# Splitting the cast of the token values and re-ordering the matrix engine in a segmented transformer with memory

## The chip, the cores and the metric

The kernel runs on one core of a Trainium2 chip. The metric is the device time of one execution in microseconds (us). A core has five engines that run in parallel and meet at semaphores: TensorE (PE, with its weight loads shown apart as PEld), VectorE (DVE), ScalarE (ACT), GpSimd (POOL) and SyncE (SP). Here SP issues nearly all of the DMAs.

## The reference

The input x has 2048 rows of 512. Attention goes through it in 64 segments of 32 tokens, one after the other, because the 8 memory rows of a segment are the first 8 output rows of the one before:

```python
for s in range(n_seg):                               # 64
    h = concat([mem, xs])                            # 8 + 32 rows of 512
    q, k, v = (einsum('btd,dhe->bhte', h, W) for W in (Wq, Wk, Wv))   # 32 heads of 128
    p = softmax(where(mask, q @ k^T * scale, -1e9))
    o = einsum('bhte,hed->btd', p @ v, Wo)
    mem = o[:, :8]; outs.append(o[:, 8:])
h  = x + A(layernorm(x))
h2 = h + gelu(layernorm(h) @ w1 + b1) @ w2 + b2      # inner size 1792
```

## The kernel before, in words

**Work of a segment on PE.** The query and key passes of both halves of the heads (Q0, Q1, K0, K1) and the value passes (V0, V1) come from `one_pass` (line 796 and, with a weight that is still loaded, line 547). Each is written in four units of four matmuls of 128x512. SC0 and SC1 are the scores of the memory rows (line 963), PV0 and PV1 their values (lines 994 and 998), PVA the values of the 24 token rows of the segment before (line 1055). WO is the output projection in eight units of eight matmuls (`wo_units`, line 1083); in a trace it is 64 matmuls. SA is the scores of token rows (line 1025). F0 and F1 are fillers: passes of a block of 4 segments whose results are needed later (hB is the tile that they read, line 796), or the output projection of a block's last rows (`wo_B`, line 1112, tile OTB, eight units of four matmuls).

**The order.** `ORDERS` is a table of strings that gives, for each place, the order of these units on PE. The places are a1 to a3 (the first segments), m0 to m3 (the segments between by their number modulo 4) and z60 to z63 (the last). "F1.0.3" stands for units 0 to 2 of F1. `TURNED` names passes that run through their four blocks backwards, so that a weight can be kept from one pass to the next. DVE, ACT, POOL and SP get their order from a list scheduler in which `BONUS` shifts priorities; it also picks ACT or DVE for operations declared with `either`. `LOCK`, `LEAD` and `PADS` insert weight loads so that instruction fetches come at set places.

**The recurrence.** WO's last matmul is followed by a transpose of its PSUM bank on DVE (tile TT, line 1095), two additions that write the memory rows into hT (line 1089), and the first Q or K matmul of the next segment, which reads them. What the table writes behind WO in a segment (fillers and SA) runs on PE beside this chain; what it writes between the first hT matmul and WO's end does not.

**Token values.** PVA leaves its result in PSUM in the tile quad; `pv_a_ev` (lines 1060 to 1064) copies it into OT with one cast of 128x768, under the key OTx. All eight WO units of a segment wait for that key.

**The start.** Lines 710 to 724 issue the first DMAs: memory rows, the bias and two blocks of x on ACT's queue, and on SP's queue WV, WK and WQ in four pieces of 1 MB each and WO in eight pieces of 512 KB. A normalised block of x is the tile xn (line 738), made on DVE from statistics (line 734) and a reciprocal root on POOL (rst, lines 736 and 737). From the third block on xn is made during the segments, one in four segments. oBn (line 1120) is a sum on DVE of the token rows of a block, also one in four segments. The statement that records it is marked `alone`, which makes the next instruction on DVE be preceded by a wait.

Of the kernel before, what the change touches and what calls it, by code (L numbers as in the profile page):

```python
# [1599 lines left out]
```

## Time and profile before

| | |
|---|---|
| median of 3 runs | 806.18 us (803.99 to 807.5) |
| the profiled execution | 803.95 us, of which its span is 802.2 us |
| mean granted PE clock | 0.998 |
| busy in the span: PE, DVE, ACT, POOL | 97%, 75%, 70%, 11% |
| DMA | 48.77 MB, 61 GB/s over the span |

In the profile a row of the timeline has the start, the time from the start of its first instruction to the end of its last, engine and line, the tiles and how many instructions are run together. The end of a matmul is modelled: rows of PE overlap, so times on PE are taken below from start to start. A bracket behind a row is idle time ahead of it and what ended it. A window row holds each engine's busy time and the clock that PE was granted.

### The profile page before, as it was taken

How to read it: one execution, taken by the hardware profiler on the slowest of the kernel's cores; microseconds unless marked ns; L12 is line 12 of the kernel's file. 1: busy time of each engine (PE TensorE's matmuls, PEld its weight loads, DVE VectorE, ACT ScalarE, POOL GpSimd, SP SyncE). 2: the span in 40 equal slices, each digit the busy share in tenths (PEclk: the TensorE clock that was granted, in tenths of full speed). 3: DMA queues.
4: the chain of work that ended last, by engine and by line, in shares of the span. 5: the costliest groups of instructions: out<-in, count | busy, mean ns of one | idle time of the engine just before them, and what ended most of it. 6: DMA issues, size and time to landing. Idle time of an engine off the chain costs nothing.

```text
span 802.2 us, 46835 instructions
## 1 busy us (share of the span) xinstructions
PE 775.9 (97%) x21699; PEld 423.1 (53%) x20880; DVE 600.7 (75%) x1847; ACT 558.0 (70%) x1580; POOL 90.1 (11%) x211
## 2 busy tenths in 40 slices
PE   2899999999999999999999999999999999999998
PEld 1455555555555555555555555555555555644444
DVE  3277878888888888888888888888888888732311
ACT  1557777777777777777778777777777777773342
POOL 5022000010001010101010101000000000020700
PEclk9999999999999999999999999999999999999999
DMA  9961010201111121102010202010212112074300
GB/s 367 394 174 24 4 37 11 45 12 37 26 33 30 30 33 27 36 19 42 19 43 15 49 12 50 13 37 20 50 25 56 51 38 59 17 232 127 86 27 26
DMA packets 65555, 48.77 MB, mean 61 GB/s; under 512 B 28996, under 2 KB 63308, under 8 KB 63820
## 3 DMA queue, kind: packets, MB, share of 16 engines
q1 hardware_dynamic: 65024, 45.50, 20.3%
q8 instruction: 166, 2.72, 1.4%
q14 instruction: 33, 0.27, 0.1%
q10 hardware_dynamic: 332, 0.27, 0.1%
HBM read 31.08 MB, written 8.13 MB: 49 GB/s over the span
## 4 chain that ended last, share of the span: by engine, by line
PE 91%; DMA 3%; DVE 2%; ACT 1%; SPq 1%; issue 1%; POOL 0%; DVEq 0%; ACTq 0%
PE ps L796 43%; PE ps L1083 15%; PE ps L547 8%; PE quad L1465 6%; PE ps L1451 5%; DMA WQ<-in_A_Wq_dram 3%; PE ps L1112 3%; PE quad L994 3%; PE quad L1055 2%; PE ps L1025 2%; PE ps L1233 1%; PE ps L963 1%; PE quad L963 1%; SPq L708 1%; PE quad L998 1%
## 5 line engine op out<-in xcount | busy, mean ns | idle before, releaser
L1083 PE MATMUL ps<-WO,OT 128*32 128x256 bf16 x4224 | 140.6, 274 | 0.1
L796 PE MATMUL ps<-WQ,hT 128*32 128x512 bf16 x1864 | 131.6, 379 | 0.7 <-DVE hT L1089 0.5
L796 PE MATMUL ps<-WV,hT 128*32 128x512 bf16 x1364 | 125.2, 381 | 0.0
L796 PE MATMUL ps<-WK,hT 128*32 128x512 bf16 x1700 | 123.6, 380 | 0.1
L815 ACT ACTIVATE kq<-ps 128x512 bf16<-128x512 f32 x160 | 95.4, 597 | 32.3 <-PE ps L796 26.4
L1083 PEld LDWEIGHTS ps<-WO,OT 128*32 128x32 bf16 x4224 | 100.9, 96 | 26.5 <-ACT OT L814 5.5
L814 ACT CAST kq<-ps 128x512 bf16<-128x512 f32 x162 | 94.8, 585 | 19.9 <-PE ps L796 13.1
L814 ACT CAST OT<-quad 128x128 bf16<-128x128 f32 x191 | 84.4, 442 | 27.0 <-PE quad L998 18.8
L839 DVE STREAM_TRANSPOSE KALL<-kq 128x256 f32<-128x256 f32 x160 | 71.2, 445 | 15.0 <-ACT kq L814 11.8
L796 PEld LDWEIGHTS ps<-WQ,hT 128*32 128x32 bf16 x1864 | 50.3, 97 | 58.8 <-issue 19.0
L861 POOL COPY ZC<-QTB 128x256 bf16<-128x256 bf16 x64 | 25.6, 401 | 477.2 <-PE ps L963 455.7
L796 PEld LDWEIGHTS ps<-WK,hT 128*32 128x32 bf16 x1700 | 45.8, 96 | 56.9 <-issue 14.5
L547 PE MATMUL ps<-WV,hT 128*32 128x512 bf16 x684 | 67.6, 379 | 0.0
L796 PEld LDWEIGHTS ps<-WV,hT 128*32 128x32 bf16 x1364 | 38.4, 97 | 47.3 <-issue 36.6
L839 DVE STREAM_TRANSPOSE QT<-kq 128x256 f32<-128x256 f32 x128 | 57.0, 445 | 6.5 <-ACT kq L815 1.9
L1454 ACT ACTIVATE WQ<-ps,b1t 128x512 bf16<-128x512 f32 x42 | 28.9, 688 | 46.6 <-PE ps L1451 46.6
L1095 DVE STREAM_TRANSPOSE TT<-ps 128x256 f32<-128x256 f32 x66 | 29.7, 450 | 36.3 <-PE ps L1083 36.1
L814 ACT CAST VS<-ps 128x512 bf16<-128x512 f32 x65 | 38.1, 586 | 26.6 <-PE ps L796 26.5
L814 DVE CAST VS<-ps 128x512 bf16<-128x512 f32 x63 | 41.8, 663 | 5.4 <-PE ps L796 5.4
L1541 DVE TENSOR_TENSOR WV<-quad,WV 128x512 bf16<-128x512 f32 (+1 forms) x16 | 10.5, 672 | 45.6 <-PE quad L1465 45.6
L982 DVE TENSOR_TENSOR PC<-EC,rsc 128x128 bf16<-128x128 f32 x128 | 39.7, 310 | 4.3
L1112 PE MATMUL ps<-WO,OTB 128*32 128x512 bf16 x512 | 42.1, 381 | 0.4 <-issue 0.2
(163 smaller groups left out, 1432.1 us busy)
## 6 DMA issues: line engine op xcount, KB each, us to landing
WV<-in_A_Wv_dram SPq DMA_DIRECT2D x4, 1024.0 KB, 8.5
WK<-in_A_Wk_dram SPq DMA_DIRECT2D x4, 1024.0 KB, 14.2
WQ<-in_A_Wq_dram SPq DMA_DIRECT2D x4, 1024.0 KB, 24.7
WO<-in_A_Wo_dram SPq DMA_DIRECT2D x8, 512.0 KB, 9.4
v_last<-VSB SPq DMA_DIRECT2D x60, 64.0 KB, 2.9
VBD<-v_last SPq DMA_DIRECT2D x60, 64.0 KB, 2.9
h_mid<-xr SPq DMA_DIRECT2D x16, 128.0 KB, 1.8
WK<-in_B_w_dram SPq DMA_DIRECT2D x4, 512.0 KB, 4.6
```

What stands on the lines that cost most here:

```text
L547: return e.add_instruction(mybir.InstMatmult(name="I-%d" % (4000000 + _kept[0]), engine=mybir.EngineType.PE, start_tensor_calc=start, stop ...
L796: ins = e.matmul(o, l, m, start=(k == 0), stop=(k == DC - 1), tile_position=(0, 32 * j), skip_group_check=True)
L814: return {"act": (lambda e: e.copy(out, src), t_act(n, ps_)), "dve": (lambda e: e.tensor_copy(out, src), 0.16 + 1.042e-3 * n * fast)}
L815: return {"act": (lambda e: e.mul(out, src, scale_), t_act(n, ps_)), "dve": (lambda e: e.tensor_scalar(out, src, scale_, None, ALU.mult), ...
L839: S.op("dve", lambda e: e.transpose(out, src), reads=[("kq", i)], writes=[key], dur=t_dve(256) + 0.02, after=after)
L982: S.op("dve", lambda e: e.tensor_tensor(PC[:, r].rearrange("p t a -> p a t"), EC[:, r], bc, ALU.mult), reads=[("EC", r), ("rsc", r)], writ ...
L1083: ins = e.matmul(ps[bank][32 * j:32 * j + 32, 0:256], lhs(slot(h)), wo_cols(h, b), start=(k == 0), stop=(k == 15), tile_position=(0, 32 * ...
L1095: S.op("dve", lambda e: e.transpose(tt.rearrange("p c q t -> p (c q t)"), ps[bank][:, 0:256]), reads=[("ps", bank)], writes=[("TT", par)], ...
L1112: ins = e.matmul(ps[bank][32 * j:32 * j + 32, :], OTB[:, bk % 2, slot(h), :], WO[:, h, :], start=(k == 0), stop=(k == 7), tile_position=(0 ...
L1451: ins = e.matmul(ps[bank][:, 0:SBT], W1[:, cc, fc * P:(fc + 1) * P], hnT_of(k)[:, cc, :], start=(cc == 0), stop=(cc == DC - 1))
L1454: S.op("act", lambda e: e.activation(gT[:, fc, :], ps[bank][:, 0:SBT], ACTF.Gelu_apprx_tanh, bias=b1t[:, fc:fc + 1], scale=1.0), reads=[(" ...
L1465: S.op("pe", lambda e: e.matmul(quad[:, t, :], lhs, W2[:, fc, :], **flags), reads=[("W2", part_of(fc))] + gT_keys(k, fc), writes=[("ps", t ...
```

## The change

1. `pv_a_ev` makes two casts of 128x384, one for each half of the heads, under the keys (OTx, half); a WO unit waits only for the half it reads.
2. WO is loaded in 16 pieces of 256 KB, and a WO unit waits only for its own two. Both blocks of x are now issued ahead of the memory rows and the bias, and these four issues are held in that order.
3. `ORDERS`, `TURNED` and `BONUS` are new throughout; LOCK is 108 for 106, LEAD 189 for 199.

```diff
-LOCK = 106
+LOCK = 108
-LATE, RAW, LEAD = 0, 12, 199
+LATE, RAW, LEAD = 0, 12, 189
...
-          "m3": "K0.0.1 Q0.0.2 K0.1.2 Q0.2.4 K0.2.4 Q1.0.4 K1.0.4 SC0.0.1 V1.0.1 V0.0.1 V1.1.2 V0.1.3 V1.2.3 V0.3.4 SC1.0.1 F1.0.1 V1.3.4 PVA.0.2 PV0.0.1 F1.1.5 WO.0.1 PV1.0.1 WO.1.8 F1.5.7 SA.0.1 F1.7.8",
+          "m3": "K0.0.1 Q0.0.2 K0.1.2 Q0.2.4 Q1.0.1 K0.2.4 Q1.1.4 K1.0.4 SC0.0.1 V1.0.1 V0.0.2 V1.1.3 V0.2.4 SC1.0.1 V1.3.4 F1.0.1 PVA.0.2 PV0.0.1 F1.1.4 WO.0.2 PV1.0.1 WO.2.8 F1.4.7 SA.0.1 F1.7.8",
...
         def first(fn, kb, writes):
-            S.dma(fn, kb, writes=writes, eng="act")
+            firsts.append(S.dma(fn, kb, writes=writes, eng="act", behind=firsts[-1] if firsts else None))
+        firsts = []
         load_x(0, first)
+        load_x(1, first)
         first(lambda e: e.dma_start(m0, A_mem0[0]), 8, ["m0"])
         first(lambda e: e.dma_start(b1n[:], b1_d), 4, ["b1n"])
-        load_x(1, first)
...
-        for g in range(4):
+        for q in range(8):
             for a in range(2):
-                h0 = 16 * (g // 2) + 8 * a + 4 * (g % 2)
-                load(lambda e, h0=h0: e.dma_start(WO[:, h0:h0 + 4, :], wo_d[:, h0:h0 + 4, :]), 590, [("WO", g, a)])
+                h0 = 16 * (q // 4) + 8 * a + 2 * (q % 4)
+                load(lambda e, h0=h0: e.dma_start(WO[:, h0:h0 + 2, :], wo_d[:, h0:h0 + 2, :]), 295, [("WO", q, a)])
...
         def pv_a_ev(s):
             opar = s % 2
-            src = quad[:, :, 256:512].rearrange("p j (k q) -> p j k q", k=8)[:, :, :, 0:NA]
-            ot = OT[:, opar, :, 0:NA].rearrange("p (j k) q -> p j k q", k=8)
-            S.either(copy2(ot, src, 768), reads=QK, writes=[("OTx", opar)])
+            for half in range(2):
+                k = slice(4 * half, 4 * half + 4)
+                src = quad[:, :, 256:512].rearrange("p j (k q) -> p j k q", k=8)[:, :, k, 0:NA]
+                ot = OT[:, opar, :, 0:NA].rearrange("p (j k) q -> p j k q", k=8)[:, :, k]
+                S.named(S.either(copy2(ot, src, 384), reads=QK, writes=[("OTx", opar, half)]), "OTx%d" % half)
...
-                S.op("pe", f, reads=[("WO", q // 2, a) for a in range(2)] + reads(q // 4), writes=[("ps", bank)], dur=0.22, mode=MC, ni=16)
+                S.op("pe", f, reads=[("WO", q, a) for a in range(2)] + reads(q // 4), writes=[("ps", bank)], dur=0.22, mode=MC, ni=16)
...
-            wo_units(lambda sl: OT[:, par, sl, :], lambda r: [("OTm", par, r), ("OTx", par)], bank)
+            wo_units(lambda sl: OT[:, par, sl, :], lambda r: [("OTm", par, r), ("OTx", par, r)], bank)
```

**The end of m3 on PE.** From PVA of an m3 segment to the last instruction ahead of the next segment's first matmul on hT, the instructions of before stand like this (a row is a run of equal instructions; WO,OTB is the filler `wo_B`, WO,OT the projection WO, KALL,QT is SA):

```order
L1055 MATMUL quad<-PTA,VS 128x32 x32
L994 MATMUL quad<-PTC,VS 128x16 x16
L998 MATMUL quad<-PTC,VBD 128x64 x4
L1112 MATMUL ps<-WO,OTB 32x512 x16
L1083 MATMUL ps<-WO,OT 32x256 x8
L994 MATMUL quad<-PTC,VS 128x16 x16
L998 MATMUL quad<-PTC,VBD 128x64 x4
L1083 MATMUL ps<-WO,OT 32x256 x56
L1112 MATMUL ps<-WO,OTB 32x512 x8
L1025 MATMUL ps<-KALL,QT 32x32 x32
L1112 MATMUL ps<-WO,OTB 32x512 x4
```

The same place of the changed kernel:

```order
L1058 MATMUL quad<-PTA,VS 128x32 x32
L997 MATMUL quad<-PTC,VS 128x16 x16
L1001 MATMUL quad<-PTC,VBD 128x64 x4
L1117 MATMUL ps<-WO,OTB 32x512 x12
L1088 MATMUL ps<-WO,OT 32x256 x16
L997 MATMUL quad<-PTC,VS 128x16 x16
L1001 MATMUL quad<-PTC,VBD 128x64 x4
L1088 MATMUL ps<-WO,OT 32x256 x48
L1117 MATMUL ps<-WO,OTB 32x512 x12
L1028 MATMUL ps<-KALL,QT 32x32 x32
L1117 MATMUL ps<-WO,OTB 32x512 x4
```

One filler unit of four matmuls has moved from ahead of WO (16 to 12) to behind it (8 to 12). In m0, m1 and m2 the number of matmuls behind WO is unchanged; there SA and the filler have only changed places.

**The end of m0 on DVE.** The last instructions of DVE before a segment boundary behind m0, before the change (KALL is a transpose for the keys):

```order
L1089 TENSOR_TENSOR opT<-TT 64x4x24 x2
L839 STREAM_TRANSPOSE KALL<-kq 128x256
L1120 TENSOR_TENSOR oBn<-OTB 32x512
L1095 STREAM_TRANSPOSE TT<-ps 128x256
L1089 TENSOR_TENSOR hT<-TT 64x4x8 x2
```

and after it:

```order
L1094 TENSOR_TENSOR opT<-TT 64x4x24 x2
L842 STREAM_TRANSPOSE KALL<-kq 128x256
L1125 TENSOR_TENSOR oBn<-OTB 32x512
L741 TENSOR_SCALAR xn<-xr,agg,rst 128x512
L1100 STREAM_TRANSPOSE TT<-ps 128x256
L1094 TENSOR_TENSOR hT<-TT 64x4x8 x2
```

The normalisation xn now stands between oBn and TT in 12 of the 14 m0 segments; before, it stood in the m3 segment ahead. Over the whole program 15 copies of 128x128 to the tile ZC (line 853) move from ACT to DVE, and 14 copies of the mask (line 938) from DVE to ACT.

**The start on POOL.** Before, the turn of OTB's mask and the identity stand around the first reciprocal root:

```order
L884 MEMSET OTB 128x608
L887 AFFINE_SELECT OTB<-OTB 128x4x8 x4
L736 TENSOR_SCALAR rst<-agg 128x1
L737 TENSOR_TENSOR rst<-rst,cneg 128x1
L656 MEMSET ident 128x128
L657 AFFINE_SELECT ident<-ident 128x128
L736 TENSOR_SCALAR rst<-agg 128x1
```

After it, the identity is made first of all, and at this place stand:

```order
L668 AFFINE_SELECT maskL<-maskL 128x16
L739 TENSOR_SCALAR rst<-agg 128x1
L740 TENSOR_TENSOR rst<-rst,cneg 128x1
L739 TENSOR_SCALAR rst<-agg 128x1
L740 TENSOR_TENSOR rst<-rst,cneg 128x1
L887 MEMSET OTB 128x608
```

Both roots have moved ahead of the work on OTB.

More of the change, by code (lines that the diff above doesn't have):

```diff
@@ L33 @@
 HOIST = 24
-LATE, RAW, LEAD = 0, 12, 199
+LATE, RAW, LEAD = 0, 12, 189
 PIECES = (0, 4, 8, 11, 14)
 HALVES = ("kq", "KA", "QT", "ZCm", "VS", "nmc", "EC", "rsc", "PC", "PTC", "OTm", "KB", "QTB", "VSB")
-BONUS = {"": 3.88, "EC0": 19.37, "EC0@a1": -40, "EC0@a2": 0, "EC0@a3": 2.13, "EC0@m0": 4.48, "EC0@m1": 40, "EC0@m2": 0, "EC0@m3": -7.71,
[48 rows of a table removed]
-         "kq4@m1": 0, "kq5": 4.41, "kq5@m0": -40, "kq5@m1": 17.96, "maskA": 40, "maskAF": 28.24, "maskCF": 40, "maskR": 4.63, "nma": -6.56,
[22 rows of a table removed]
+BONUS = {"": 0.43, "EC0": 12.67, "EC0@a1": -13.59, "EC0@a2": 7.92, "EC0@a3": 40, "EC0@m0": 16.73, "EC0@m1": 14.92, "EC0@m2": -3.63, "EC0@m3": 40,
[50 rows of a table added]
+         "kq5": 3.19, "kq5@m0": 16.46, "kq5@m1": -3.01, "maskA": 40, "maskAF": 28.24, "maskCF": 40, "maskR": 4.63, "nma": -1.25, "nma@a1": 14.79,
[22 rows of a table added]
 LEAN = 0.36
@@ L117 @@
          ("SA", 0, 99))
-TURNED = {"a1": "K0 Q1 V0", "a2": "K0 Q0", "a3": "V1", "m0": "F0 F1 Q0 V0", "m1": "K0 K1 Q1 V0", "m2": "F0 K0 K1 V0", "m3": "F1 K0 K1 Q1 V0", "z60": "F1 K0 K1 V0 V1", "z61": "Q0 Q1 V0", "z62": "F1 K0 Q0", "z63": "K0 K1 V0 V1"}
-ORDERS = {"a1": "Q0.0.3 K1.0.1 Q0.3.4 K0.0.2 Q1.0.1 K0.2.4 Q1.1.4 K1.1.4 SC0.0.2 V0.0.3 V1.0.1 V0.3.4 V1.1.2 SC1.0.1 V1.2.4 PVA.0.2 PV0.0.1 F1.0.1 WO.0.2 PV1.0.1 WO.2.8 F1.1.2 SA.0.1 F1.2.4",
[10 rows of a table removed]
+TURNED = {"a1": "K1 Q0 Q1", "a2": "K0 K1 Q1 V0 V1", "a3": "Q0 V0", "m0": "F0 Q1 V0", "m1": "F0 K0 K1 Q1 V0", "m2": "F0 K0 K1 Q0 V0", "m3": "F0 K0 K1 Q1 V0", "z60": "F1 K1 Q0 V0", "z61": "Q0 V0 V1", "z62": "F1 Q0 V0", "z63": "Q0 Q1 V0 V1"}
+ORDERS = {"a1": "Q0.0.2 Q1.0.1 Q0.2.4 K1.0.1 K0.0.4 Q1.1.4 K1.1.4 SC0.0.2 V0.0.1 V1.0.1 V0.1.4 V1.1.2 SC1.0.1 V1.2.4 F1.0.1 PVA.0.2 PV0.0.1 WO.0.2 PV1.0.1 WO.2.8 F1.1.4 SA.0.1",
[10 rows of a table added]
 BANK = dict(K0=7, K1=4, Q0=6, Q1=5, V0=5, V1=6, F0=4, F1=5, FB=5, SC0=0, SC1=7, SA=4, WO=6)
@@ L695, in build_kernel @@
         S.op("pool", lambda e: e.memset(opT[:], 0.0), writes=["opT0"] + [("opA", i, k) for i in range(2) for k in range(4)], dur=1.0)
-        S.op("dve", lambda e: e.memset(OT[:], 0.0), writes=[("OTm", p, r) for p in range(2) for r in range(2)] + [("OTx", p) for p in range(2)], dur=1.0)
+        S.op("dve", lambda e: e.memset(OT[:], 0.0), writes=[("OTm", p, r) for p in range(2) for r in range(2)] + [("OTx", p, r) for p in range(2) for r in range(2)], dur=1.0)
         def load_x(tb, load=S.dma):
@@ L1114, in f @@
                     return ins
-                S.op("pe", f, reads=[("WO", g, a) for g in range(4) for a in range(2)] + [("OTB", bk % 2, sg) for sg in range(4)], writes=[("ps", bank)], dur=0.216, mode=MC, ni=8)
+                S.op("pe", f, reads=[("WO", q, a) for q in range(8) for a in range(2)] + [("OTB", bk % 2, sg) for sg in range(4)], writes=[("ps", bank)], dur=0.216, mode=MC, ni=8)
             okeys = [("OTB", bk % 2, sg) for sg in range(4)]
```

160 rows, old and new, of tables (BONUS, ORDERS) are left out of this document.

## The prediction

> **What bounds the kernel now.** I read the page's first and fourth part, then the timeline at three segment boundaries, then the first 50 us.
>
> ```profile
> PE 775.9 (97%) x21699; PEld 423.1 (53%) x20880; DVE 600.7 (75%) x1847; ACT 558.0 (70%) x1580; POOL 90.1 (11%) x211
> ...
> PE 91%; DMA 3%; DVE 2%; ACT 1%; SPq 1%; issue 1%; POOL 0%; DVEq 0%; ACTq 0%
> ```
>
> PE is the bound: busy for 97% and 91% of the chain that ended last. The change has the same number of matmuls, so it can gain only in the few per cent where PE waits. Two places are of that kind: the boundary between segments and the start. First the end of an m1 segment and the start of the next, PE alone:
>
> ```profile
> 389.39 0.82 PE L796 MATMUL ps<-WQ,hB 128*32 128x512 bf16 x12
> 390.04 0.40 PE L1025 MATMUL ps<-KALL,QT 128*32 128x32 bf16 x32
> 390.26 0.41 PE L796 MATMUL ps<-WQ,hB 128*32 128x512 bf16 x4
> 390.55 0.61 PE L796 MATMUL ps<-WK,hT 128*32 128x512 bf16 x8
> ```
>
> From the first instruction behind WO (389.39) to the first hT matmul (390.55) it is 1.16 us. That is the recurrence: TT and the two hT additions on DVE. What stands in between is covered by it: 12 filler matmuls take 0.65 (0.054 each), SA 0.22, and the last four begin 0.29 ahead of hT though they need 0.22. So in m1 sixteen fillers and SA fit, with 0.07 left. Now the end of m3, all engines (PE's weight loads, SP and POOL left out):
>
> ```profile
> 368.17 0.80 ACT L814 CAST OT<-quad 128x768 bf16<-128x768 f32 x1
> 368.73 0.41 DVE L738 TENSOR_SCALAR xn<-xr,agg,rst 128x512 bf16<-128x512 bf16 x1 [1.00 <-POOL rst L737]
> ...
> 368.87 0.89 PE L1112 MATMUL ps<-WO,OTB 128*32 128x512 bf16 x8
> ...
> 369.10 0.45 DVE L1095 STREAM_TRANSPOSE TT<-ps 128x256 f32<-128x256 f32 x1
> ...
> 369.38 0.59 PE L1025 MATMUL ps<-KALL,QT 128*32 128x32 bf16 x32
> 369.58 0.39 DVE L1089 TENSOR_TENSOR hT<-TT 64x32 bf16<-64x32 f32 x2
> ...
> 369.80 0.41 PE L1112 MATMUL ps<-WO,OTB 128*32 128x512 bf16 x4
> ...
> 370.03 1.26 PE L796 MATMUL ps<-WQ,hT 128*32 128x512 bf16 x20
> ```
>
> Again 1.16 us (368.87 to 370.03), with only twelve fillers and SA in it. Four more matmuls should fit as they do in m1. But SA takes 0.42 here (369.38 to 369.80), not 0.22, and the eight fillers ahead of it 0.51 where 0.43 would do: PE paused for 0.08 in them and SA then went at half its pace. In another m3 neither is the case:
>
> ```profile
> 451.43 0.60 PE L1112 MATMUL ps<-WO,OTB 128*32 128x512 bf16 x8
> 451.86 0.40 PE L1025 MATMUL ps<-KALL,QT 128*32 128x32 bf16 x32
> 452.09 0.41 PE L1112 MATMUL ps<-WO,OTB 128*32 128x512 bf16 x4
> 452.58 0.40 PE L796 MATMUL ps<-WQ,hT 128*32 128x512 bf16 x4
> ```
>
> Here SA takes 0.23, and the four fillers begin 0.49 ahead of hT (0.22 of work, 0.27 spare). Of the 14 m3 boundaries eight are of the first kind (a pause of 0.02 to 0.35 in the fillers, and SA 0.42), two of the second, and in four SA takes 0.37 to 0.38 and the last fillers begin about 0.35 ahead of hT.
>
> **The change part by part.** *One OTB unit of m3 behind WO.* It takes 4 x 0.054 = 0.22 us away from ahead of WO. Where SA is short the spare 0.27 takes it in, and the segment is 0.22 shorter. With 0.35 ahead of hT, 0.35 - 0.22 = 0.13 is spare, and the segment is 0.13 shorter. Where the fillers pause and SA keeps its 0.42, the last fillers begin only 0.23 ahead of hT: 0.01 is spare, and what goes ahead of WO comes back behind it. 2 x 0.22 + 4 x 0.13 + 8 x 0.01 = **-1.0 us**. Ends: -3.1 (14 x 0.22, if no pause falls there any more, as in most m1) and 0 (if one falls in each).
>
> *xn between oBn and TT in twelve m0.* The usual m0 boundary, DVE and PE:
>
> ```profile
> 378.39 0.68 DVE L1120 TENSOR_TENSOR oBn<-OTB 32x512 bf16<-32x512 f32 x1
> ...
> 379.10 1.04 PE L796 MATMUL ps<-WK,hB 128*32 128x512 bf16 x16
> ...
> 379.39 0.45 DVE L1095 STREAM_TRANSPOSE TT<-ps 128x256 f32<-128x256 f32 x1 [0.33 <-PE ps L1083]
> ...
> 379.88 0.39 DVE L1089 TENSOR_TENSOR hT<-TT 64x32 bf16<-64x32 f32 x2
> ```
>
> oBn ends at 379.07 and TT waits 0.33 for PE. The xn of 0.41 (the row of m3 above) is longer than that hole. Late in the program the trace holds the new order itself, with another line's xn of the same shape:
>
> ```profile
> 584.68 0.68 DVE L1120 TENSOR_TENSOR oBn<-OTB 32x512 bf16<-32x512 f32 x1
> ...
> 585.46 0.41 DVE L1224 TENSOR_SCALAR xn<-xT,agg,rst 128x512 bf16<-128x512 bf16 x1
> 585.79 0.44 DVE L1095 STREAM_TRANSPOSE TT<-ps 128x256 f32<-128x256 f32 x1
> ```
>
> There TT starts 0.43 behind oBn's end (585.36), 0.10 later than 0.33. hT follows TT and the first Q or K follows hT, so 0.10 goes straight into the segment: the PE work behind WO is unchanged and was already covered. 12 x 0.10 = **+1.2 us**. The lower end is 0, if oBn starts earlier; the upper is 0.2 each, +2.4, if one of the 15 ZC copies that come to DVE (219 ns each in their group) pushes oBn:
>
> ```profile
> L853 DVE COPY ZC<-QT 128x128 bf16<-128x128 bf16 x64 | 14.0, 219 | 0.1
> ```
>
> What goes from m3 there gives nothing back: xn ended (369.14) when TT could start anyway. The two other m0, where oBn's extra wait ahead of TT also goes, give about 0.07 each, -0.1.
>
> *The split cast.* Two casts of 128x384 for one of 128x768. The nearest row is a copy of that size out of PSUM:
>
> ```profile
> 16.98 0.48 ACT L814 COPY hT<-quad 128x384 bf16<-128x384 bf16 x1
> ```
>
> 2 x 0.48 against 0.80 adds 0.16 us to ACT in each segment. ACT is 70% busy, and the cast of this segment (368.17, beside WO) is read by WO of the next one, some 10 us on. **0**; were each to delay the cast that follows and so PV1 by its 0.16, 63 x 0.16 = +10, but no row shows PE waiting for OTx in a middle segment. That half of the WO units may start on half of the tokens gains nothing for the same reason.
>
> *Other orders of m0 to m2, a1, a3 and the last places.* Same units, moved within stretches that PE fills without a hole: 0. In a3 PVA no longer stands ahead of the last V, -0.2 at most. The four oN writes now issued ahead of the transpose of xT on SP have several us until they are read. 0.
>
> *The start.* Rows of the first 50 us:
>
> ```profile
> 9.88 0.69 DVE L734 BATCH_NORM_STATS2 stt<-xr 128x6 f32<-128x512 bf16 x1 [6.82 <-DMA xr<-in_A_x_dram]
> ...
> 15.75 0.23 DVE L738 TENSOR_SCALAR xn<-xr,agg,rst 128x512 bf16<-128x512 bf16 x1
> ...
> 17.11 3.65 PE L796 MATMUL ps<-WV,hB 128*32 128x512 bf16 x32 [0.47 <-ACT hB L814]
> ...
> 28.24 1.91 PE L796 MATMUL ps<-WK,hB 128*32 128x512 bf16 x32
> ...
> 33.47 0.82 PE L796 MATMUL ps<-WQ,hB 128*32 128x512 bf16 x12
> ...
> 35.34 0.40 PE L796 MATMUL ps<-WQ,hB 128*32 128x512 bf16 x4 [1.05 <-DMA WQ<-in_A_Wq_dram]
> ...
> 47.30 0.62 PE L1083 MATMUL ps<-WO,OT 128*32 128x256 bf16 x16
> ```
>
> With x first, and POOL's roots ahead of the OTB work, xn can come some 4 to 5 us earlier, and V with it. But the fourth piece of WQ lets PE go on only at 35.34, and the chain of waits shows that this is a transfer of its own:
>
> ```profile
> 7.24 28.05 DMA WQ<-in_A_Wq_dram
> ```
>
> The bytes ahead of it are the same, so it lands at 35.3 again; what comes earlier ahead of it only lengthens that wait. WQ's 4 MB at the windows' 414 to 424 GB/s take about 10 us, so WK lands near 25.3, and the K passes at 28.24 can come up by 2.9 us: the wait of 1.05 becomes about 3.9. Behind it WO's eight pieces (16 now, same bytes) end near 47: from there at most some tenths are to be had (the 0.35 between 47.30 and the last matmuls). What a long wait does to PE's clock is in the windows:
>
> ```profile
> 32.20:35.60 3.40, 2.35 (x48) 0.98 (x44) 1.34 (x3) 1.51 (x3) 0.00 (x0) 1.00 1.03 362
> 35.60:39.00 3.40, 2.73 (x52) 1.14 (x44) 1.30 (x3) 2.70 (x6) 0.00 (x0) 1.00 1.10 348
> 39.00:42.40 3.40, 1.77 (x68) 0.82 (x68) 2.35 (x11) 2.61 (x14) 1.14 (x3) 1.00 1.10 352
> 42.40:45.80 3.40, 3.23 (x88) 2.21 (x92) 1.62 (x5) 1.39 (x5) 0.00 (x0) 0.50 1.10 349
> ```
>
> After a window with PE busy for 1.77 of 3.40 the next has clock 0.50; after 2.35 and 2.73 it keeps 1.00. With 3.9 us of waiting, 31.4 to 35.3, the window of 32.20 has almost no work, so the one of 35.60 should have clock 0.50. Its 2.73 of work is the Q passes, on the chain to WO: up to half of it, 1.4 us, is lost. **+1.2 us**, with ends -0.35 (no loss, and the last pieces of WO taken sooner) and +2.8 (two windows). The Trainium skill, "TensorE: Matmul & The Clock Gate", Part 1, gives such a rule: a free-running window of 3413 ns, half rate after an idle one. The windows here agree in length and clock; by its table an idle window is needed, so that 1.77 of work in a window would not have halved the clock, and the trace shows that it did. By that table the window of 32.20, in which some 0.3 of work is left, would keep the clock too and the sum would be 806.1 without this term; I go by the row.
>
> *LOCK, LEAD, pads.* They move instruction fetches; stalls of 0.1 to 0.6 that I saw in the fillers of some m1 and m3 may come elsewhere: 0, within 0.5 either way.
>
> **The sum.** -1.0 + 1.2 - 0.1 - 0.2 + 1.2 = +1.1 us on the profiled execution's 803.95 (span 802.2 and 1.75 around it): 805.05. The median of the runs shown is 2.2 higher, 806.18, and so I give 807.3 for a median of such runs.
>
> **The rivals.** (1) *m3's gain comes in full and nothing else matters:* no pause in m3's fillers, TT's 0.10 hidden, the clock kept. -3.1 - 0.3 - 0.35 = -3.8, so 802.4. For it: the m1 rows hold the same work in 1.16. Against it: SA's 0.42 and the two rows at 585.46 and 585.79. (2) *DVE becomes the bound at m0:* if the chain of DVE operations ahead of oBn ends 0.26 later than now, TT no longer waits for PE at all, and all of xn's 0.41 plus a ZC copy's 0.22 lie on the recurrence: 12 x 0.63 = 7.6 instead of 1.2. 807.3 + 6.4 = 813.7, slower. It decides at 0.26 us: that is how long oBn's end now stands ahead of what TT needs (0.33 less the start of 0.07). For it: DVE is 75% busy and in m0 without a hole; against it, TT alone shows a wait of 0.33. (3) *The start gives what its parts promise:* V 4.8 earlier and all behind it too, 801.3. Against it stands the 28.05 of WQ. (4) *The clock at half for two windows:* 807.3 + 1.6 = 808.9. (5) *Nothing but names changes*, the m3 unit finds no room, xn finds its hole and the clock is kept: 806.2, within a fraction of the forecast.
>
> **How the numbers follow.** What a measurement of this kernel can tell from no change is about 0.5%, 4 us: 802.1 to 810.2 counts as the same. Chances: the forecast (with 5) 0.50, of which 0.05 fall beyond either edge together by the runs' own scatter (803.99 to 807.5); (1) 0.20, near the lower edge, half beyond; (2) 0.13, nearly all beyond; (3) 0.06, beyond; (4) 0.11, a fifth beyond. So faster 0.18, same 0.64, slower 0.18. The range reaches from 801.8, below (1), to 811.0, past (4) and short of the full (2).
>
> **What would show it.** In the changed profile: at m3's ends, twelve fillers, SA and four fillers between WO and hT in 1.16 (gain) or 1.3 and more (none); xn 0.1 behind oBn at m0 and TT 0.43 behind it; the wait for WQ grown from 1.05 to about 3.9 but its end again at 35.3; a window of clock 0.50 that begins there; the first hT matmul behind the first WO at 49 to 50.5. I am wrong if WQ lands earlier, or if the boundaries of m0 to m2 differ by more than 0.1 from 1.16.

## The result, and the profile after

The changed kernel takes 808.39 us in the median of 15 runs (805.79 to 809.88), the kernel before 804.65 us in as many runs beside it (802.42 to 809.05). The ratio is 1.0039 with a 95% interval of 1.0024 to 1.0053: slower by about 3.1 us, and within the 0.5% that the prediction counted as no change. (Ratios, here and below, are worked out from all the runs and are not the quotient of the two medians, which lie 3.7 us apart here. One run of e9, of 888.8 us at a mean clock of 0.853, is left out.) The profiled execution takes 805.79 us (span 804.1), 1.84 more than the one of before. Its page begins as before, and PE is as busy:

```profile
PE 776.0 (97%) x21683; PEld 421.0 (52%) x20865; DVE 591.2 (74%) x1850; ACT 567.3 (71%) x1641; POOL 87.5 (11%) x211
...
PE 92%; DMA 3%; ACT 1%; DVE 1%; SPq 1%; issue 1%; DVEq 0%; ACTq 0%
```

So the difference is again in PE's waits. I measured it at 64 points: the start of the first matmul on hT of each segment. Against before it is 2.16 us late at the end of segment 0 (51.19 us for 49.03), 1.87 late at the end of segment 3, 1.66 at the last one. **All of the loss of this execution is in the first segment; the rest gives 0.5 us back.** The two rows of segment 0's end, before and after:

```profile
49.03 1.02 PE L796 MATMUL ps<-WQ,hT 128*32 128x512 bf16 x12
51.19 1.26 PE L799 MATMUL ps<-WQ,hT 128*32 128x512 bf16 x20
```

For the middle I cut each segment in two: the stretch from the first hT matmul to the last WO matmul, and the boundary from there to the next hT matmul (the chain over DVE). Medians of 14 segments each, in us, from the start times of PE's matmuls:

| | m0 work | m1 work | m2 work | m3 work | boundary behind m0 | m1 | m2 | m3 |
|---|---|---|---|---|---|---|---|---|
| before | 8.97 | 8.97 | 8.97 | 9.17 | 1.325 | 1.26 | 1.25 | 1.255 |
| after | 9.025 | 8.97 | 8.98 | 8.97 | 1.42 | 1.37 (1.25 at best) | 1.25 | 1.255 |

A median hides what happens in a few segments of the 14. Behind m1 and m3 single boundaries are longer, by stops of PE that are treated below. In segment 4, the first m0, the work is 9.47 us for 8.98, and 9.34 or more in all variants of the changed kernel: PV0 waits there for DVE, where PA (the probabilities of the token rows) and its transpose now run just ahead of PC, from which PV0's operand is made.

```profile
88.33 0.27 PE L997 MATMUL quad<-PTC,VS 32*128 32x16 bf16 x16 [0.36 <-DVE PTC L986]
```

An end of m3, of the changed kernel, PE and DVE:

```profile
369.98 0.82 PE L1117 MATMUL ps<-WO,OTB 128*32 128x512 bf16 x12
370.21 0.45 DVE L1100 STREAM_TRANSPOSE TT<-ps 128x256 f32<-128x256 f32 x1 [1.26 <-PE ps L1088]
...
370.63 0.40 PE L1028 MATMUL ps<-KALL,QT 128*32 128x32 bf16 x32
...
370.86 0.41 PE L1117 MATMUL ps<-WO,OTB 128*32 128x512 bf16 x4
...
371.14 0.61 PE L799 MATMUL ps<-WQ,hT 128*32 128x512 bf16 x8
```

It is 1.16 us from 369.98 to 371.14, as before, with sixteen fillers and a short SA (0.23) in it. The unit that was moved is covered here. It is so in eight of the 14; in the other six SA takes 0.32 to 0.42 and the boundary is 0.03 to 0.40 us longer than 1.255. Before, four were longer, by 0.08 to 0.28. The end of m0:

```profile
379.56 0.68 DVE L1125 TENSOR_TENSOR oBn<-OTB 32x512 bf16<-32x512 f32 x1
...
380.34 0.41 DVE L741 TENSOR_SCALAR xn<-xr,agg,rst 128x512 bf16<-128x512 bf16 x1
...
380.67 0.44 DVE L1100 STREAM_TRANSPOSE TT<-ps 128x256 f32<-128x256 f32 x1
```

oBn ends at 380.24; xn starts 0.10 and TT 0.43 behind it, without a wait for PE. This order stands in nine of the 14 m0 segments of the trace (segments 12 to 44), not in twelve: three of the twelve xn run earlier, at 62 to 79 us, as three did before. And the start, PE alone, then the windows:

```profile
32.64 0.40 PE L799 MATMUL ps<-WQ,hB 128*32 128x512 bf16 x4 [2.09 <-DMA WQ<-in_A_Wq_dram]
35.19 0.62 PE L799 MATMUL ps<-WQ,hB 128*32 128x512 bf16 x4 [2.15 <-DMA WQ<-in_A_Wq_dram]
...
40.56 0.31 PE L966 MATMUL ps<-KALL,ZC 128*32 128x64 bf16 x16 [1.05 <-POOL ZC L864]
...
42.82 0.26 PE L997 MATMUL quad<-PTC,VS 32*128 32x16 bf16 x16 [0.63 <-DVE PTC L986]
...
44.93 0.28 PE L997 MATMUL quad<-PTC,VS 32*128 32x16 bf16 x16 [1.80 <-DVE PTC L986]
```

```profile
32.20:35.60 3.40, 0.81 (x12) 0.25 (x16) 0.00 (x0) 0.00 (x0) 0.00 (x0) 0.84 1.03 361
35.60:39.00 3.40, 3.40 (x48) 1.43 (x44) 1.11 (x3) 1.76 (x4) 0.00 (x0) 0.66 1.10 347
39.00:42.40 3.40, 1.99 (x60) 0.68 (x52) 2.34 (x7) 2.02 (x8) 1.14 (x3) 1.00 1.10 351
42.40:45.80 3.40, 1.18 (x80) 0.98 (x84) 1.57 (x7) 2.06 (x9) 0.00 (x0) 0.85 1.10 348
45.80:49.20 3.40, 3.40 (x72) 2.28 (x65) 2.47 (x7) 1.22 (x3) 0.00 (x0) 0.65 0.80 239
```

PE waits 4.2 us for WQ where it waited 1.05, and goes on at the same time (35.19 for 35.34). Then the clock is low. The values between 0.5 and 1 come from where the windows are cut. With other cuts the trace shows two stretches of 3.41 us at 0.50, with 1.00 between them:

```profile
34.52:37.94 3.42, 2.75 (x28) 1.08 (x32) 0.45 (x1) 0.97 (x2) 0.00 (x0) 0.50 1.10 348
41.35:44.76 3.41, 1.16 (x36) 0.40 (x28) 2.05 (x8) 2.38 (x11) 0.40 (x1) 1.00 1.11 349
44.76:48.18 3.42, 3.25 (x89) 2.15 (x93) 2.00 (x6) 1.05 (x3) 0.00 (x0) 0.50 1.03 309
```

The kernel before has one, from 42.40 to 45.81. The scores are 1.0 us later than before (40.56 for 39.55), and PV1 is 2.36 later (44.93 for 42.57): a second loss of 1.3 lies between PV0 and PV1, where PE waits 1.80. The rows of ACT show it:

```profile
41.75 0.20 ACT L979 ACTIVATION_READ_ACCUMULATOR EC<-ps,nmc 128x1 f32 x1
42.25 0.60 ACT L818 ACTIVATE kq<-ps 128x512 bf16<-128x512 f32 x1 [0.30 <-PE ps L799]
42.88 0.38 ACT L941 COPY ps<-maskAF 128x256 f32<-128x256 f32 x1
43.19 0.27 ACT L817 CAST OT<-quad 128x128 bf16<-128x128 f32 x1
43.36 0.32 ACT L979 ACTIVATE EC<-ps,nmc 128x64 f32<-128x64 f32 x1
```

The second exponential (EC, for the second half of the heads) stands behind the next block's query evacuation, a mask copy and the cast of the first half; before, all four exponentials ran in one piece, and the evacuation came behind the last of them:

```profile
41.12 0.32 ACT L976 ACTIVATE EC<-ps,nmc 128x64 f32<-128x64 f32 x1
...
41.41 0.61 ACT L815 ACTIVATE kq<-ps 128x512 bf16<-128x512 f32 x1
```

PE's hole from 43.1 to 44.9 leaves it 1.16 us of work between 41.35 and 44.76, and the second low stretch of the clock follows.

The profiled execution is the fastest of the 15. A stretch of 3.41 us at half rate takes 0.002 off the mean clock of an execution (half of 3.41 in 804). Six of the 15 runs have a mean clock of 0.996, which is two stretches, as in the profile, and take 807.6 us in the mean; nine have 0.992 to 0.994, which is three or four, and take 808.9. In the 85 runs of the kernel before beside the experiments it is 0.995 to 1.000, two stretches at most.

### The profile page after: what moved, and what is told of

Read it like the earlier page. It is cut to its first block, busy times and chain, and to the rows that moved or that the text cites. A ratio compares the mean times of both kernels' runs of the same rounds, so it can differ in the third digit from the quotient of the medians.

```text
span 804.1 us, 46875 instructions
## 1 busy us (share of the span) xinstructions
PE 776.0 (97%) x21683; PEld 421.0 (52%) x20865; DVE 591.2 (74%) x1850; ACT 567.3 (71%) x1641; POOL 87.5 (11%) x211
## 4 chain that ended last, share of the span: by engine, by line
PE 92%; DMA 3%; ACT 1%; DVE 1%; SPq 1%; issue 1%; DVEq 0%; ACTq 0%
PE ps L799 43%; PE ps L1088 15%; PE ps L549 9%; PE quad L1470 6%; PE ps L1456 5%; DMA WQ<-in_A_Wq_dram 3%; PE ps L1117 3%; PE quad L997 3%; PE quad L1058 2%; PE ps L1028 2%; PE ps L1238 1%; PE quad L966 1%; PE ps L966 1%; SPq L710 1%; PE quad L1001 1%
## 5 line engine op out<-in xcount | busy, mean ns | idle before, releaser
L799 PE MATMUL ps<-WQ,hT 128*32 128x512 bf16 x1748 | 128.7, 382 | 0.9 <-DVE hT L1094 0.6
L799 PE MATMUL ps<-WK,hT 128*32 128x512 bf16 x1740 | 127.0, 379 | 0.1
L817 ACT CAST OT<-quad 128x384 bf16<-128x384 f32 (+1 forms) x254 | 94.3, 371 | 29.2 <-PE quad L1001 19.2
L799 PEld LDWEIGHTS ps<-WK,hT 128*32 128x32 bf16 x1740 | 48.2, 97 | 56.1 <-issue 19.8
L799 PEld LDWEIGHTS ps<-WQ,hT 128*32 128x32 bf16 x1748 | 47.2, 97 | 57.0 <-issue 15.7
L1040 ACT ACTIVATE SA<-SA 128x256 f32<-128x256 f32 x64 | 26.7, 417 | 26.6 <-DVE SA L1039 25.3
L799 PE MATMUL ps<-WQ,hB 128*32 128x512 bf16 x512 | 39.5, 393 | 4.4 <-DMA WQ<-in_A_Wq_dram 4.2
```

Source lines behind the costliest of these rows:

```text
L799: ins = e.matmul(o, l, m, start=(k == 0), stop=(k == DC - 1), tile_position=(0, 32 * j), skip_group_check=True)
L817: return {"act": (lambda e: e.copy(out, src), t_act(n, ps_)), "dve": (lambda e: e.tensor_copy(out, src), 0.16 + 1.042e-3 * n * fast)}
L1040: exps[:] = [S.named(S.op("act", lambda e: e.activation(SA[:], SA[:], ACTF.Exp), reads=["SA"], writes=["SA"], dur=t_act(256, False)), "SAe")]
```

## The experiments

Theory A: the loss is at the start, 1.0 us by the clock and 1.3 by ACT's order; in the middle m3 gives 2.8, xn takes about 1 and a later score in m0 0.8. Its rivals are named with each run. Times are medians; ratios are to the kernel before, run on the same chip.

**e1: the loads alone**, in the kernel before.

```diff
         load_x(0, first)
+        load_x(1, first)
         first(lambda e: e.dma_start(m0, A_mem0[0]), 8, ["m0"])
         first(lambda e: e.dma_start(b1n[:], b1_d), 4, ["b1n"])
-        load_x(1, first)
...
-                load(lambda e, h0=h0: e.dma_start(WO[:, h0:h0 + 4, :], wo_d[:, h0:h0 + 4, :]), 590, [("WO", g, a)])
+                load(lambda e, h0=h0: e.dma_start(WO[:, h0:h0 + 2, :], wo_d[:, h0:h0 + 2, :]), 295, [("WO", q, a)])
...
```

> The kernel before with the new loads alone: x ahead of the small inputs and chained, WO in 16 pieces, each WO unit waiting for its own two. The orders and casts are those of before. Theory A (the loss at the start comes from the order of work on ACT and from PE's clock, not from the loads): xn stays behind the KALL memset, so V starts near 17.1 us, the wait for WQ stays near 1.0 us, the first memory rows are there at 49.0 us give or take 0.3, and the time is that of before within 0.15% (ratio 0.9985 to 1.0015). Rival B (the 16 smaller pieces or the earlier x make WQ or WO land later): the wait for WQ or the one ahead of the last WO units grows by 1 us or more and the ratio is 1.0015 to 1.004.

Measured: 806.13 us, ratio 0.9990 (0.9976 to 1.0004). The total is as theory A has it, the details are not: V does start earlier, and PE waits longer for WQ and then runs at a low clock here too.

```profile
32.66 0.40 PE L797 MATMUL ps<-WQ,hB 128*32 128x512 bf16 x4 [0.99 <-DMA WQ<-in_A_Wq_dram]
35.30 0.40 PE L797 MATMUL ps<-WQ,hB 128*32 128x512 bf16 x4 [2.24 <-DMA WQ<-in_A_Wq_dram]
```

```profile
35.60:39.00 3.40, 3.40 (x40) 1.33 (x36) 0.89 (x2) 1.85 (x5) 0.00 (x0) 0.53 1.10 348
...
42.40:45.80 3.40, 2.53 (x120) 1.80 (x116) 2.31 (x8) 2.38 (x10) 0.00 (x0) 1.00 1.11 349
```

But with ACT's order of before the last WO units start at 47.12 (47.30 before). The stretch that lost its clock is only an earlier one, 35.83 to 39.25: before, it was that from 42.40. The first hT matmul comes at 49.80, 0.77 later than before and outside of the 49.0 give or take 0.3 that was expected; what stands between is a stop of PE among the padding matmuls ahead of it, with no wait that the profile knows:

```profile
49.36 0.61 PE L766 MATMUL ps<-WV,ident 128*32 128x512 bf16 x8 [1.18 <-issue]
```

By the ratio the smaller pieces and the earlier x do neither harm nor good. Rival B's cause, a later landing, does not show: WQ's fourth piece lets PE go on at 35.30, and WO's last units start earlier.

**e2: the m3 unit alone**, in the kernel before.

```diff
-"m3": "... PV0.0.1 F1.1.5 WO.0.1 PV1.0.1 WO.1.8 F1.5.7 SA.0.1 F1.7.8",
+"m3": "... PV0.0.1 F1.1.4 WO.0.2 PV1.0.1 WO.2.8 F1.4.7 SA.0.1 F1.7.8",
```

> The kernel before with one unit of four filler matmuls of m3 moved from ahead of WO to behind it, as the change does; nothing else is edited, though the list scheduler answers by moving xn off the end of m3 into the middle of m0. Theory A (the unit is covered at the boundary): PE work between the first hT matmul and the end of WO in m3 falls by 0.20 us at an unchanged boundary of 1.25, 14 times, -2.8 us, ratio 0.9965 with an interval of about 0.0015 to either side. Rival C (pauses of PE in the fillers give it back, as the prediction had it): the boundary behind m3 grows to 1.35 or more in over half of the cases, the sum is -1.0 us or less, ratio 0.9985 to 1.000.

Measured: 812.92 us, ratio 1.0080 (1.0052 to 1.0108), slower than either has it. The work of m3 is 8.97 in the median, 14 times -0.20 as theory A says. The boundary behind m3 is not unchanged: six of the 14 are 1.35 or more, the longest 2.11, and their sum is 20.7 us for 18.3 before. That gives back 2.4 of the 2.8. So in this execution m3 is nearer to rival C, though C expected it in over half of the cases. And the work of m0 has risen to 9.41 us, +0.44 a time:

```profile
378.32 0.37 PE L1055 MATMUL quad<-PTA,VS 32*128 32x32 bf16 x32
379.04 0.27 PE L994 MATMUL quad<-PTC,VS 32*128 32x16 bf16 x16 [0.35 <-DVE PTC L983]
```

From PVA to PV0 it is 0.72 us, where it was 0.29 (375.79 to 376.08 in the kernel before). The moved unit changed the due times, and the list scheduler put xn and PA into other places on DVE in m0. The edit that was to do one thing alone did two; e11 and e12 take them apart.

**e3: one cast again**, in the changed kernel.

```diff
-            for half in range(2):
-                k = slice(4 * half, 4 * half + 4)
...
-                S.named(S.either(copy2(ot, src, 384), reads=QK, writes=[("OTx", opar, half)]), "OTx%d" % half)
+            S.named(S.either(copy2(ot, src, 768), reads=QK, writes=[("OTx", opar, half) for half in range(2)]), "OTx0")
```

> The changed kernel with the token values again leaving PSUM in one cast of 128x768, and all WO units waiting for it; all orders are those of the change. Theory A (the cast is off the path): ACT falls by about 10 us of busy time, all boundaries and the work between them are as in the changed kernel within 0.02 us, and the time is that of the changed kernel, ratio to before 1.003 to 1.005. Rival D (the added 0.16 us of ACT per segment is what makes the change slower): the time falls to that of before or below, ratio 0.999 to 1.001.

Measured: 809.58 us, ratio 1.0034 (1.0018 to 1.0049), the ratio of the changed kernel. The work of m0 to m3 is within 0.01 us of the changed kernel's, and ACT's busy time falls by 8 us (567.3 to 559.2). The boundary behind m3 is not within 0.02 as expected; its median is 1.35, by stops of PE. No cost of the split can be seen: D falls.

**e4: xn behind TT**, in the changed kernel.

```diff
-                 reads=[("xr", tb % XR), ("ag", i), ("rs", i)], writes=[("xn", i)], dur=0.38)
+                 reads=[("xr", tb % XR), ("ag", i), ("rs", i)], writes=[("xn", i)], dur=0.38, after=behind)
...
-                ln1(bk + 3)
+                ln1(bk + 3, [S.last_writer[("hTm", s % RING)]])
```

> The changed kernel with xn of the third block and later made to wait for the memory rows of m0, so that it stands behind TT on DVE, in m1. Theory A (xn between oBn and TT costs 0.1 us a time): the boundary behind m0 falls from 1.42 to 1.325 in twelve places, -1.1 us in all, and nothing else moves; ratio to before 1.002 to 1.0035. Rival E (xn costs nothing where it stands, or as much in m1): the boundary behind m0 or the work in m1 keeps the 0.1, and the time is that of the changed kernel.

Measured: 808.95 us, ratio 1.0020 (1.0003 to 1.0037). The boundary behind m0 falls from 1.42 to 1.324 in the nine segments concerned, and the work of m1 stays within 0.02:

```profile
382.67 0.45 DVE L1100 STREAM_TRANSPOSE TT<-ps 128x256 f32<-128x256 f32 x1 [0.33 <-PE ps L1088]
```

So xn did cost its 0.1 a time, 0.9 us in all, and it costs nothing in m1. In the ratio this can't be told from the changed kernel's 1.0039, since the intervals overlap. The profiled execution is longer than the changed kernel's (span 807.6 for 804.1), by stops of PE, most of them in m3, that are treated below.

**e5: the exponential first**, in the changed kernel: the evacuation of the first pass of the second block's queries waits for it.

```diff
-            S.either(copy2(kq[:, i], ...), reads=[("ps", bank)], writes=[("kq", i)])
+            S.either(copy2(kq[:, i], ...), reads=[("ps", bank)], writes=[("kq", i)], after=hold)
...
+                                hold[:] = [S.last_writer[("EC", 1)]] if (what, b, r) == ("Q", 1, 0) else []
                                 kq_B(b, "KQ".index(what), r, bank)
...
```

> The changed kernel with one order on ACT at the start put back: the second exponential of segment 0 runs ahead of the evacuation of the next block's queries, the mask copy and the first cast to OT, as it does in the kernel before. Theory A (of the 2.2 us that the start is late, 1.3 are that order and 1.0 the clock): the gap between the first and the second PV of segment 0 falls from 2.1 us to about 0.8, and the first memory rows come at 49.9 us for 51.2; the whole 1.3 us earlier. Rival F (everything waits for the last pieces of WO or for the clock anyway): the second PV comes earlier but WO's end stays within 0.4 us of where it was.

Measured: 803.09 us, ratio 0.9998 (0.9987 to 1.0010). **This one order on ACT takes the whole loss away.** On ACT, DVE and POOL nothing differs from the changed kernel but the places of three instructions on ACT and of one on DVE. PE, ahead of WO:

```profile
43.10 0.26 PE L998 MATMUL quad<-PTC,VS 32*128 32x16 bf16 x16 [0.36 <-DVE PTC L987]
...
43.92 0.27 PE L998 MATMUL quad<-PTC,VS 32*128 32x16 bf16 x16 [0.51 <-ACT OT L817]
...
47.20 0.64 PE L1089 MATMUL ps<-WO,OT 128*32 128x256 bf16 x16
48.92 1.47 PE L799 MATMUL ps<-WQ,hT 128*32 128x512 bf16 x20
```

The gap of the two PV is 0.82 us as expected, but the hT matmul comes 2.27 earlier and not 1.3. The windows tell why:

```profile
35.60:39.00 3.40, 3.40 (x40) 1.40 (x36) 0.89 (x2) 1.76 (x4) 0.00 (x0) 0.55 1.10 348
...
42.40:45.80 3.40, 2.53 (x117) 1.73 (x113) 2.44 (x9) 2.40 (x10) 0.00 (x0) 1.00 1.10 347
45.80:49.20 3.40, 3.15 (x85) 2.13 (x79) 2.93 (x9) 0.74 (x2) 0.00 (x0) 1.00 0.83 245
```

With the hole gone, the window of 42.40 holds 2.53 of work instead of 1.18, and the one behind it keeps clock 1.00 instead of 0.65. The hole cost its own length and a second time through the clock. Rival F falls. The wait for WQ and the low stretch behind it (35.91 to 39.32) are still there, and yet hT comes 0.11 earlier than in the kernel before, which has its one low stretch later: here and in e1 the new wait only moves that stretch.

**e6: the clock kept**, in the changed kernel, by 16 groups of four matmuls whose results nobody uses.

```diff
+                                if (what, b) == ("Q", 0) and r == 0:
+                                    warm(7, 16)
+                                    u = S.pe_order[-20:]
+                                    S.pe_order[-20:] = u[:2] + u[4:10] + u[2:3] + u[10:] + u[3:4]
```

> The changed kernel with 16 extra groups of four matmuls on the identity while PE waits for WQ: six ahead of WQ's third piece, ten ahead of its fourth (results unused). The insertion also moves padding weight loads in the segments behind it. Theory A (the wait halves PE's clock and that costs 1.0 us): the granted clock stays at 1.0 between 32 and 39 us, the first scores of segment 0 come about 1.0 us earlier (39.5 for 40.56), and so do the first memory rows. Rival G (the clock isn't what makes Q late): the clock stays up, but scores come no more than 0.3 us earlier; or the extra matmuls make the fourth piece's matmuls late.

Measured: 805.84 us, ratio 1.0028 (1.0017 to 1.0039). The clock is kept and the scores come at 39.48, 1.08 earlier, hT at 50.21, 0.98 earlier, all as theory A says; G falls. The other low stretch, behind the hole on PE, stays (43.91 to 47.33). The ratio can't be told from the changed kernel's, since the intervals overlap; the 1 us is read from the profiles.

```profile
32.20:35.60 3.40, 2.73 (x48) 1.21 (x52) 0.00 (x0) 0.00 (x0) 0.00 (x0) 1.00 1.03 364
35.60:39.00 3.40, 2.82 (x52) 1.18 (x44) 1.91 (x4) 2.29 (x5) 0.07 (x1) 1.00 1.11 350
```

**e7: ZC copies as before**, in the changed kernel: in m0 the first on ACT, the second on DVE.

```diff
...
+            if s > 3 and s % 4 == 0 and r == 0 and s < NS - 4:
+                del alts["dve"]
+            if s > 3 and s % 4 == 0 and r == 1 and s < NS - 4:
+                del alts["act"]
...
```

> The changed kernel with the first half's ZC copy of each m0 made on ACT and the second half's on DVE, as before the change. Theory A (two ZC copies on DVE make the scores of m0 0.05 us late): PE work between the first hT matmul and the end of WO in m0 falls from 9.025 to 8.97 us, 14 times, -0.8 us. Rival H (the 0.05 comes from the order of Q and K on PE in m0): it stays at 9.02 or more.

Measured: 812.16 us, ratio 1.0108 (1.0091 to 1.0125). The work of m0 rises from 9.025 to 9.32: worse than either theory. On ACT the copy now stands behind a query evacuation (377.44 to 378.04), and the scores wait for it:

```profile
377.93 0.30 ACT L856 COPY ZC<-QT 128x128 bf16<-128x128 bf16 x1
...
378.37 0.31 PE L971 MATMUL quad<-KALL,ZC 128*32 128x64 bf16 x16 [0.17 <-ACT ZC L856]
```

**e8: e5 and e4 together.** 

> The changed kernel with both repairs that worked alone: the second exponential of segment 0 ahead on ACT, and xn behind TT. Theory A (the start and xn are separate losses and add up): first memory rows at 48.9 us, boundary behind m0 1.325, so 1.2 us less than with the first repair alone, which stood at 0.9998 of before: ratio 0.998 to 0.9995. Rival I (scattered pauses of PE decide more than these terms): the boundaries are as said, but the ratio is 1.000 or above because the sum of the pauses, 1 to 5 us in the profiles so far, comes out high.

Measured: 805.37 us, ratio 0.9991 (0.9976 to 1.0005). The boundary behind m0 is 1.325 as expected, but hT comes first at 49.50 (two low stretches in a row there, 33.45 to 40.28), and the profiled execution has stops of 7.7 us in all against e5's 1.7. No difference from before can be seen, nor one from e5: rival I is nearer.

**e9: e5 and e6 together.** 

> The changed kernel with the second exponential of segment 0 ahead on ACT and the 16 extra groups that keep PE's clock up while it waits for WQ. Theory A (WO's last pieces, near 47.2 us, are a floor under the start): the scores of segment 0 come 1 us earlier than with the first repair alone (39.6 for 40.8), but the last WO units still start at 47.0 to 47.4, now waiting for a DMA, and the first memory rows come at 48.6 to 49.0. Rival J (no such floor): they come at 47.9 or earlier, and the time falls by 1 us more.

Measured: 806.83 us, ratio 1.0008 (0.9991 to 1.0026). The scores come at 39.26, but the last WO units at 47.60 and hT at 49.27: no gain over e5. It is not a DMA that they wait for, as theory A had it:

```profile
39.00:42.40 3.40, 1.91 (x85) 1.01 (x88) 2.49 (x10) 2.81 (x13) 0.86 (x3) 0.90 1.10 348
42.40:45.80 3.40, 3.34 (x94) 2.07 (x86) 2.17 (x7) 1.42 (x5) 0.00 (x0) 0.59 1.10 354
```

```profile
46.39 0.83 PE L1089 MATMUL ps<-WO,OT 128*32 128x256 bf16 x22 [0.65 <-issue]
```

The clock falls later, from 41.74 to 45.16, behind a stretch in which the chain of scores leaves PE 1.69 of 3.41 us of work. With the pause of 0.65 in WO (the second view, PE's timeline) beside it, the microsecond is spent again in this execution. That can't be the whole reason: four of the nine runs in the ratio have a mean clock of 1.000, so no low stretch, and take 806.9 us in the mean against 807.3 for the other five. Why e9 gains nothing stays open, and so does whether WO's loads are a floor, since no profile came early enough to touch it.

**e10: m0's order of Q and K as before**, in the changed kernel; a single run.

```diff
-"m0": "Q0.0.3 Q1.0.1 Q0.3.4 K0.0.3 Q1.1.2 K0.3.4 Q1.2.4 K1.0.4 ...
+"m0": "Q0.0.2 Q1.0.1 Q0.2.4 K0.0.4 Q1.1.4 K1.0.4 ...
```

> The changed kernel with the order of Q and K passes of m0 as before the change (K0 in one piece ahead of the rest of Q1); the list scheduler moves further instructions on DVE in m0 in answer, xn among them. Theory A (in the changed m0 the transpose of K0's result comes late on DVE, since K0 ends two units later on PE and stands behind a ZC copy and PA): the last K pass of m0 is followed by the scores after 0.86 us again, not 0.91. Rival K (the copy of ZC on DVE alone does it): 0.91 stays.

Measured: 814.01 us. The last K pass is followed by the scores after 0.863 us again (0.913 in the changed kernel), as theory A says, though both ZC copies stay on DVE in all but two of the m0 segments. So K falls. But the scheduler's answer moved PA from ahead of the first K transpose to behind the second, as in e2, and the work of m0 is 9.40. Whether the 0.05 comes from K0 ending later on PE or from PA standing ahead of its transpose is not separated.

**e11 and e12: taking e2 apart.** e11 is e2 with e4's edit; e12 adds a wait of the first K transpose of m0 for PA (JOIN is 0 in this kernel, so the old list was empty).

```diff
...
-[zc[r]] if JOIN & 1 and s > 0 else ()
+[S.last_writer["PA"]] if 3 < s < NS - 4 and s % 4 == r == 0 else ()
...
```

> The kernel before with the m3 unit behind WO, as in e2, and xn made to wait for the memory rows of m0, so that it no longer stands in the middle of m0. In e2 the PE work of m0 rose from 8.97 to 9.41 us, 14 times, with PVA waiting. Theory L (xn of 0.4 us in the middle of m0's chain on DVE causes that): m0 falls back to 8.97, and the time is that of before less 2.8 us, ratio 0.995 to 0.998. Rival M (it is PA, the token rows' probabilities, which the scheduler put behind the second K transpose in e2, so that PVA is late): m0 falls only in part, to 9.05 to 9.3, and the ratio is 0.998 to 1.005.

Measured: 815.00 us, ratio 1.0089 (1.0053 to 1.0124). The work of m0 is 9.41, with xn gone from there. So xn was not the cause, and L falls; of M the culprit fits, but not the partial fall that it expected, there was none.

> As e11, and the first K transpose of each m0 made to wait for PA, so that PA and its transpose stand ahead of it on DVE again; the scheduler answers by moving oBn into the middle of m0. Theory M (PA late was e2's loss): PVA no longer waits in m0, PE work of m0 is 8.97 to 9.05, the boundary behind m0 falls from 1.325 to 1.26 since oBn no longer stands ahead of TT, and the ratio is 0.994 to 0.998. Rival N (what is moved ahead of the scores of m0 makes them late instead): PE work of m0 stays at 9.2 or more.

Measured: 818.61 us, ratio 1.0160 (1.0136 to 1.0184). The work of m0 is 10.10, 1.13 more than in the kernel before: the scores now come 0.49 later, and from PVA to PV0 it is 0.92 instead of 0.29. The boundary behind m0 did fall to 1.254, with oBn gone from ahead of TT. Rival N: what was moved ahead made the scores late. That PA's late place is what costs e2 its 0.44 is the likeliest reading (in e2 PA and its transpose run ahead of the first PC on DVE, 0.41 and 0.31 us), but no run shows it by itself. Segment 4 of the changed kernel, where the two run at that place too, loses about as much (0.49). No version here beats the kernel before by more than its interval.

## Why the prediction was right, and where its steps were not

- **The sum**: +1.1 forecast; the profiled executions differ by 1.84, the ratio stands for 3.1 us. The direction and the range held. That the sum came so near is in part luck: in these executions m3 gave about 1.5 more and xn took 0.3 less than forecast, while the start took 1.0 more and m0, put at 0, took 1.2.
- **m3's unit**: -1.0 forecast. In work it is -2.8 (14 x 0.20), in every profile with the unit moved. What the ends give back differs: the 14 boundaries behind m3 add up to 18.3 us before and 18.4 in e1, where the unit was not moved; to 18.3 to 18.6 in the changed kernel, e5, e6 and e7; and to 19.6 to 21.4 in e2, e3, e4 and e8 to e12. So the net was -2.5 in the changed kernel's profile, and over all twelve about -1.3. The step was mis-sized for this pair: it took a long SA, with or without a pause in the fillers, to come again at twelve of the 14 ends, and in the profile after it is at six. As a reason it was sound: in e2 and others the ends gave most of the gain back. With one profile of each kernel it stays open whether the kernel or the execution decides this.
- **xn between oBn and TT**: +1.2 forecast from the two rows at 585 us. TT stands 0.43 behind oBn as there, the boundary is 0.10 longer, and e4 takes it away. The price was right and the count was not: nine places, so +0.9. The -0.1 for two other m0 did not come; their boundary stays at 1.33.
- **The split cast and the smaller pieces of WO**: 0 forecast; e1 and e3 agree within their intervals.
- **m0's work**: the prediction put the other orders at 0. It is 0.055 a time, +0.8 us, and 0.4 more in segment 4. The 0.055 goes with the order of K0 and with PA's place on DVE (e10), and which of the two it is stays open.
- **The start**: +1.2 forecast, +2.16 found. The wait for WQ (3.9 forecast, 4.2 found), its end (35.3, 35.19) and the low clock behind it were right, and so was the price of a low stretch (1.2 forecast, 1.0 by e6). What failed is the step from there to a loss: the term was added to a start that already had a low stretch at 42.40. In e5, with ACT's order of before, that one goes away, and hT comes at 48.92 for 49.03. What I left out is that ACT's order there also changed, with the second exponential behind three others; by e5 this was worth 2.3 us with the second low stretch that it brings. The chain's 1% of ACT did not point to it; a comparison of the order of ACT's instructions at the start would have.
- **Of the rivals**, (2) did not come: the boundary behind m0 is 0.10 longer and not 0.63. (3) fell as argued: x earlier only lengthened the wait for WQ. (4), two windows at half rate, came in another form: the second stretch is not next to the first, and it follows the hole that ACT's order leaves. Two in a row, as (4) has it, stand behind WQ in e7 (33.09 to 39.92) and e8. The 808.9 of (4) is nearer to the median of 808.39 than the forecast of 807.3 is.
- **Of the signs**, the first hT matmul at 51.19 lies outside of 49 to 50.5. The limit of 0.1 from 1.16 for the boundaries of m0 to m2 was set against the forecast's own term: m0 stood at 1.23 before, by the rows from the first instruction behind WO, and xn's 0.10 had to make it 1.33.

The pauses deserve a word, since they set much of the scatter. They are stops of up to 1.2 us with no wait that the profile knows. Over the 56 middle segments, what work and boundaries take beyond their undisturbed length adds up to 2.8 us in the profile before, 3.0 after, 6.6 in e3, 7.1 in e4, 1.7 in e5, 7.7 in e8, most of it in m3 and m1. In the waits of PE in e8 some have a row of their own:

```profile
PE quad L1059 <- issue: 2.7, 4, 0.8
```

Four stops ahead of PVA, 0.8 us the longest. As before and after are nearly equal here, the pauses do not explain the 1.84 between the two profiles. What the changed kernel is slower by beyond that may be pauses, or the third and fourth low stretches that nine of its runs have; neither is shown. In e3, whose runs have two or four such stretches, the two kinds differ by only 0.1 us.

## What to carry to other kernels

When a hand-written order and a list scheduler are tuned together, compare the instructions of each engine at the few places that wait, the start among them: one exponential behind three other instructions on ACT cost 2.3 us here, more than all the rest of the change gave back. A hole on PE is paid twice where it empties a clock window, so look at the granted clock in the window behind it. And an edit of one unit in such a program is not one edit, since the scheduler answers elsewhere (e2, e7, e10 and e12 end 6 to 13 us behind the kernel before, e10 by a single run).

## What the runs showed of the hardware that I had not expected

- In these profiles the clock is granted at 0.50 for whole stretches of 3.41 us, or at 1.00; values between come from windows cut across the edges. A low stretch follows one in which PE has less work, but no sharp border shows. Low stretches came behind 0.40 and 1.16 of 3.41 us of work (after), 0.93 (e1, e5), 1.69 (e9), 1.77 (before) and 2.09 (e12). The clock stayed at 1.00 behind 1.69 (e5, 29.08 to 32.50), 1.78 (e3, 28.76 to 32.17) and 2.20 (after, e1). So the busy time that the profile gives, with its modelled ends of matmuls, does not decide it alone. The Trainium skill ("TensorE: Matmul & The Clock Gate", Part 1) ties half rate to an idle window; here more than half a window of work did not prevent it.
- Filling such a wait with matmuls that nobody uses keeps the clock (e6) and brought the first hT matmul 1.0 us forward; together with e5's order it brought nothing (e9).
- Where PE paused in the fillers at an end of m3, the SA behind it took 0.42 us instead of 0.22 in the profile before, in all eight cases. At the ends of m1 this held in one of five.
